# GpSimd's weight work at the head of an attention step, and another order of loads, banks and copies in steps 0 to 3

## The chip, the cores and the metric

The kernel runs on one core of a Trainium2 chip. The time is that of one execution on the device in microseconds (us), as the median of the runs shown. A core has five engines that each work through their own list of instructions in order, and wait for each other by semaphores: TensorE (PE: matrix products, and PEld, which loads their stationary operand), VectorE (DVE), ScalarE (ACT), GpSimd (POOL) and SyncE (SP, which here only issues DMAs). PE writes to PSUM, of which this kernel uses eight banks; DVE and ACT read it out.

## The reference

Causal attention for 4 batches of 12 heads, 448 tokens, head size 64, and behind it a layer with a cosine:

```
scores = q @ k.T / sqrt(64), masked above the diagonal      # per head
attn   = softmax(scores);  x = attn @ v                     # x: (1792, 768)
h   = x @ w_in                                              # (768, 2048)
out = (h * cos(h)) @ w_out                                  # (2048, 768)
```

q, k and v are float32. The weights come as 64-bit floats, two 32-bit words each, and are turned into pairs of float32 parts ("hi" and "lo") on the chip.

## The kernel before, in words

The 48 heads are handled as 24 **pairs** of heads. The function `attention` is a generator; its loop (L489) makes one **step** per iteration and gives control back (`yield`) at the end of each. In step i three pairs are in work, so that no engine waits for one pair's whole chain:

- PE: the scores of pair i (`scores`, L359), the products with v of pair i-2 (`av`, L409), the transposes of q and k of pair i+2 (`transpose_in`, L315), the transposes of the probabilities of pair i-1 (`tp`, L392), the transposes of the output of pair i-2 (`turn_out`, L447). That is its order within a step.
- DVE: masking with the row minimum for pair i (`masked`, seven custom instructions, L368), the division for pair i-2 (`divide`, L436 to L438), and one or two copies of `tp`'s result out of PSUM (`evac_tp`, L319).
- ACT: two copies of the transposed q and k of pair i+1 (`evac_in`, L321), seven exponentials (`exps`, L375), two or three copies of `evac_tp` (L321), two copies for the output of pair i-2 (`finish`, L463 and L464).
- POOL: splits that output into hi and lo (`finish_hi`, L469 and L470).
- SP: four loads of q and k for pair i+3 (`load_qk`, L257) and two of v for pair i-1 (`load_v`, L266), every second step two more of v (L273).

Beside this, between steps (L1342 to L1375), the first weights are prepared in 12 **pieces**, each over two steps. In the first half of a piece DVE makes `ct` from the high words (L139, L142), and POOL squares the high words in place (`hif`, L145). In the second half DVE adds the low words (L148) and multiplies by the test of the squared words against a bound (L152): so **L152 reads what POOL's L145 wrote**. Then POOL makes hi and lo of the result (L156, L157). DVE's part stands in the program at the `yield`, hence ahead of the next step's `masked`. POOL's part is kept in the list `postponed` and issued at the end of the next step, behind that step's `finish_hi` (L557):

```
# in convert_weight, half 0:
    return lambda: nc.gpsimd.tensor_tensor(hif, hif, hif, op=ALU.mult), None
# at the end of a step:
    finish_hi(i - 2, xf)
    while postponed:
        postponed.pop(0)()
    yield i
```

SP also loads the pieces (L117, L122), writes finished weights back to DRAM (`first_halves`, L204 and L206: they wait for POOL's L156 and L157) and raw ones (L1344, behind L152). The pieces start in step 2 and end in step 26. Nothing reorders any of this: the program is recorded under a manual schedule, so each engine's order is that of the Python code.

Ahead of step 0, q and k of pair 0 are transposed with products on zeros (`keep_warm`, L286) before, between and behind. From step 23 on, products of the second part (L567 to L569) fill PE; then the function `moe` runs (from L635), in which PE works almost without a break.

Of the kernel before, what the change touches and what calls it, by code (L numbers as in the profile page):

```python
# [21 lines left out]
def kernel(  # L22
# [15 lines left out]
    nc = tc.nc  # L38
# [189 lines left out]
    def attention(filler_of, postponed):  # L228
        with (
# [6 lines left out]
            NM = S // R  # L236
# [4 lines left out]
            N = len(pairs)  # L241
# [4 lines left out]
            def heads(j):  # L246
                return slice(j * D, (j + 1) * D)

            def half(h):
                return slice(h * R, (h + 1) * R)  # L250

            def load_qk(i, *engs):
                b, hp = pairs[i]
                nat[i] = nat_t[:, i % 3]
                for h, src in ((1, k), (0, q)):
                    for j, eng in enumerate(engs or (nc.sync, nc.sync)):
                        eng.dma_start(  # L257
                            out=nat[i][half(h), :, heads(j)],
                            in_=src[b, 2 * hp + j].rearrange("(p c) d -> p c d", c=NM),
                        )  # L260

            def load_v(i):
                b, hp = pairs[i]
                vn, vo = vals[i] = vn_t[i % 3], vo_t[i // 2 % 2]
                for j in range(2):
                    nc.sync.dma_start(  # L266
                        out=vn[:, :, j, 0:D],
                        in_=v[b, 2 * hp + j, 0:W, :].rearrange("(c p) d -> p c d", p=P),
                    )
                if i % 2 == 0:  # L270
                    for a in range(2):
                        t0 = (LAST[a][1] - 1) * R
                        nc.sync.dma_start(  # L273
                            out=vo[R:P, a].rearrange("p g h e -> p (g h) e")[:, :, 0:D],
                            in_=v[b, 2 * hp : 2 * hp + 4, t0 : t0 + R, :].rearrange("h p d -> p h d"),
                        )
# [3 lines left out]
            load_qk(0, nc.sync, nc.scalar)  # L280
            nc.scalar.copy(cst.tile([P, 32], BF16, name="tab")[:, 0:1], warm[:, 0:1])
            load_qk(1, nc.sync, nc.scalar)

            def keep_warm(n):
                for _ in range(n):
                    nc.tensor.matmul(  # L286
                        banks8[:, 0, 0:P], lhsT=warm, rhs=warm, start=True, stop=True
                    )

            keep_warm(30)  # L290
            ident = cst.tile([P, P], F32, name="ident")
            make_identity(nc, ident)

# [16 lines left out]
            def transpose_in(i, bs, order=None):  # L310
                for h in range(2):
                    qkt[i, h] = flat[:, 2 * h + i % 2, 0:S], banks8[:, bs[h], 0:S]
                for c, h in order or [(c, h) for c in range(NM) for h in range(2)]:
                    o = qkt[i, h][1].rearrange("p (r c) -> p c r", c=NM)
                    nc.tensor.transpose(o[:, c], nat[i][half(h), c], ident[half(h), half(h)])  # L315

            def evac(dst, src, dve=False):
                if dve:
                    nc.vector.tensor_copy(dst, src)  # L319
                else:  # L320
                    nc.scalar.copy(dst, src)  # L321

            def evac_in(i, h, dve=False):
                evac(*qkt[i, h], dve)
# [11 lines left out]
            def col(m):  # L336
                return slice(COL[m], COL[m] + 1)

            def open_step(i):
                prob[i] = prob_t[i % 3]  # L340
                stats[i] = at.tile([P, 8], F32, tag="stat", bufs=3, name="stat")

            def place(m):
                b, o = BANK[m]
                return banks8[:, b, o * R : (o + m) * R]

            def probs(i, m):
                return prob[i][:, AT[m] * R : (AT[m] + m) * R]
# [16 lines left out]
            def masked(i, *ms):  # L365
                for m in ms:
                    z = W if m == TURNED else S - m * R
                    nc.vector.tensor_tensor_reduce(  # L368
                        out=probs(i, m), in0=place(m), in1=mask[:, z : z + m * R], scale=-scale,
                        scalar=3.0e38, op0=ALU.add, op1=ALU.min, accum_out=stats[i][:, col(m)],  # L370
                    )

            def exps(i, *ms):
                for m in ms:
                    nc.scalar.activation(  # L375
                        probs(i, m), probs(i, m), AF.Exp, scale=-1.0, bias=stats[i][:, col(m)]
                    )
# [7 lines left out]
            def open_ptr(i):  # L385
                ptr[i] = at.tile([P, 2, 2, NM, R], F32, tag="pm", bufs=2, name="pm")
# [87 lines left out]
            def fill(n):  # L474
                if not extra:
                    spare = itertools.cycle((7, 6))
                    extra.append(filler_of(lambda: banks8[:, next(spare)]))
                for _ in zip(range(n), extra[0]):
                    pass

            TB_, G1, G2 = (2, 3), (7, 4), (5, 6)
            transpose_in(0, TB_, [(c, 1) for c in range(NM)])
            evac_in(0, 1)
            keep_warm(8)
            transpose_in(0, TB_, [(c, 0) for c in range(NM)])
            evac_in(0, 0, True)
            keep_warm(8)
            load_qk(2)
            for i in range(N + 4):  # L489
                cur, prev, old = i < N, 0 < i <= N, 0 <= i - 2 < N  # L490
                if i >= N - 1:
                    G1, G2 = (2, 3), (4, 5)
                if i + 3 < N:
                    load_qk(i + 3)
                if prev:
                    load_v(i - 1)
                if cur:
                    open_step(i)
                    scores(i)
                if i == 0:  # L500
                    masked(i, 4, 3)
                    exps(i, 4, 3)
                    masked(i, 7, 6)
                    exps(i, 7)
                    transpose_in(1, TB_)
                    evac_in(1, 0, True)
                    evac_in(1, 1)
                    keep_warm(8)
                    exps(i, 6)
                    masked(i, 5, 1, 2)  # L510
                    exps(i, 5, 1, 2)
                    yield i
                    continue
                if i == 1:
                    transpose_in(2, TB_)
                    keep_warm(8)
                    masked(i, 4, 3, 7, 6)
                    evac_in(2, 0, True)
                    masked(i, 5)
                    evac_in(2, 1, True)  # L520
                    masked(i, 1, 2)
                    exps(i, 4, 3)
                elif cur:
                    if i + 1 < N:
                        evac_in(i + 1, 0, i == 2)
                        evac_in(i + 1, 1, i == 2)
                    masked(i, 4, 3, 7, 6, 5, 1, 2)
                    exps(i, 4, 3, 7, 6, 5, 1, 2)
                if i == N + 2:
                    run(extra[0])  # L530
                if old:
                    av(i - 2)
                    divide(i - 2)
                if 1 < i < N - 2:
                    transpose_in(i + 2, TB_)
                if i == N:
                    fill(8)
                if prev:
                    open_ptr(i - 1)
                    tp(i - 1, 0, G1)  # L540
                    evac_tp(i - 1, 0, G1, 0, True)
                    evac_tp(i - 1, 0, G1, 1)
                    if i == 1:
                        exps(i, 7, 6)
                    tp(i - 1, 1, G2)
                    evac_tp(i - 1, 1, G2, 1)
                    evac_tp(i - 1, 1, G2, 0, i % 2 == 0 or i < 4)
                if i == 1:
                    exps(i, 5, 1, 2)
                    transpose_in(3, TB_)  # L550
                if N - 2 < i < N + 2:
                    fill((4, 4, 6)[i + 1 - N])
                if old:
                    turn_out(i - 2)
                    xf = finish(i - 2)
                    finish_hi(i - 2, xf)
                while postponed:  # L557
                    postponed.pop(0)()
                yield i

    def m1_sum(ring, g, fi, t0, n, hv):
# [64 lines left out]
    def run(*gens):  # L626
        for x in gens:
            for _ in x:
                pass
# [699 lines left out]
    with tc.manual_schedule():  # L1329
# [11 lines left out]
        postponed = []  # L1341
# [65 lines left out]
```

## Time and profile before

| what | value |
|---|---|
| time, median of 3 runs | 630.5 us (625.94, 630.5, 631.62) |
| profiled execution: its time / its span | 629.74 us / 627.8 us |
| granted TensorE clock, mean | 0.997 |
| PE busy | 595.1 us (95%) |
| DVE busy | 454.3 us (72%) |
| ACT busy | 402.9 us (64%) |
| POOL busy | 399.0 us (64%) |
| attention steps 0 to 23 begin | 8.17 to 161.83 us |

The span runs from the first to the last instruction; the run's own time is 1.9 us longer. Busy shares are means over very different stages. The part that the change touches is the first 200 us, in which steps follow each other every 5.4 to 8.5 us; a step is cut here at the first instruction of its scores. "Busy" for PE counts a product from its start to a modelled end, so a burst of products that stops and starts again shows more busy time than the same burst in one go.

### The profile page before, as it was taken

What the parts mean: (1) busy time and instruction counts of PE and PEld (TensorE: products, weight loads), DVE (VectorE), ACT (ScalarE), POOL (GpSimd) and SP (SyncE); (2) the same over time, 40 slices, a digit from 0 to 9 for tenths busy, and PEclk for the clock granted to TensorE, in tenths of its full rate; (3) what the DMA queues carried; (4) which work ended last, traced back from release to release, by engine and by line L of the source; (5) the groups of instructions that cost most, each with busy time, mean ns of one, the idle gap of its engine ahead of it and who ended that gap; (6) DMA issues with size and microseconds to landing.
All of it is one profiled execution on the core that took longest, in us unless ns stands there. A gap on an engine that the chain in (4) does not pass through costs nothing.

```text
span 627.8 us, 15322 instructions
## 1 busy us (share of the span) xinstructions
PE 595.1 (95%) x5912; PEld 547.1 (87%) x5912; DVE 454.3 (72%) x957; ACT 402.9 (64%) x783; POOL 399.0 (64%) x426
## 2 busy tenths in 40 slices
PE   8898888886998999999999999999999999999996
PEld 7777777775877998889999999999999999999996
DVE  4877777667638678688777777764358877887886
ACT  3878888867657679687777777743436545644640
POOL 0233343443344978787777777772578788889895
PEclk9999999999999999999999999999999999999999
DMA  8666655754604786978796969669998567548204
GB/s 147 163 141 165 152 139 149 165 129 116 162 3 143 251 307 190 361 238 324 224 329 222 337 199 354 228 231 375 392 363 296 163 241 271 178 160 304 95 1 151
DMA packets 127096, 134.30 MB, mean 214 GB/s; under 512 B 75152, under 2 KB 111360, under 8 KB 127024
## 3 DMA queue, kind: packets, MB, share of 16 engines
q1 hardware_dynamic: 119328, 106.92, 55.2%
q0 software_dynamic: 4928, 24.78, 10.8%
q10 hardware_dynamic: 2768, 1.64, 1.0%
q8 instruction: 46, 0.75, 0.5%
q14 instruction: 26, 0.21, 0.1%
HBM read 83.36 MB, written 49.94 MB: 212 GB/s over the span
## 4 chain that ended last, share of the span: by engine, by line
PE 64%; DVE 20%; ACT 6%; POOL 4%; DMA 3%; issue 3%; SPq 0%; ACTq 0%; DVEq 0%; POOLq 0%
PE banks L663 16%; PE banks L1112 12%; PE banks L1092 11%; DVE pb L368 7%; PE banks L568 5%; PE banks L569 5%; PE banks L567 5%; DVE pm L319 2%; PE banks L409 2%; PE banks L1129 2%; PE banks L1016 2%; DVE on L438 2%; DMA land<-in_moe_w_in_dram 2%; PE banks L359 1%; POOL xa L470 1%
## 5 line engine op out<-in xcount | busy, mean ns | idle before, releaser
L651 DVE TENSOR_TENSOR acc<-acc,banks 128x768 f32<-128x768 f32 (+1 forms) x122 | 112.6, 932 | 43.0 <-PE banks L663 32.9
L663 PE MATMUL banks<-w,gh 128*128 128x384 f32 x512 | 110.3, 336 | 2.5 <-DVE acc L649 1.6
L663 PEld LDWEIGHTS banks<-w,gh 128*128 128x128 f32 x512 | 90.7, 188 | 5.0 <-DVE acc L649 2.0
L375 ACT ACTIVATE pb<-pb,stat 128x256 f32<-128x256 f32 (+6 forms) x168 | 71.8, 498 | 32.5 <-DVE stat L368 32.1
L568 PE MATMUL banks<-xa,w 128*128 128x512 f32 x192 | 75.3, 392 | 0.0
L569 PE MATMUL banks<-xa,w 128*128 128x512 f32 x192 | 75.0, 391 | 0.0
L567 PE MATMUL banks<-xa,w 128*128 128x512 f32 x192 | 74.9, 390 | 0.0
L469 POOL CAST xa<-xf 128x448 fp32r<-128x448 f32 (+1 forms) x18 | 9.7, 539 | 89.0 <-ACT xf L464 89.0
L663 PE MATMUL banks<-w,gl 128*128 128x384 f32 x256 | 65.2, 335 | 0.0
L368 DVE CUSTOM_DVE_ANT_0 pb<-banks,mask 128x256 f32<-128x256 f32 (+6 forms) x168 | 59.8, 418 | 2.6 <-PE banks L359 2.6
L687 POOL TENSOR_TENSOR w<-ct,w 128x768 fp32r<-128x768 f32 x28 | 51.8, 1850 | 15.3 <-ACT w L686 10.0
L575 ACT ACTIVATE ni<-banks 128x512 int32<-128x512 f32 (+1 forms) x64 | 34.5, 538 | 32.6 <-PE banks L569 19.6
L594 POOL TENSOR_TENSOR gl<-r,gh 128x512 fp32r<-128x512 f32 x32 | 41.5, 1298 | 19.0 <-ACT gh L593 18.8
L409 PE MATMUL banks<-vn,pm 128*64 128x65 f32 (+1 forms) x1344 | 49.5, 226 | 1.7 <-ACT xf L464 1.5
L577 DVE SCALAR_TENSOR_TENSOR r<-ni,banks 128x512 f32<-128x512 int32 (+1 forms) x56 | 35.0, 626 | 21.1 <-ACT ni L575 20.3
L409 PEld LDWEIGHTS banks<-vn,pm 128*64 128x64 f32 (+1 forms) x1344 | 45.6, 140 | 3.8 <-ACT xf L464 1.8
L579 ACT ACTIVATE r<-r 128x512 f32<-128x512 f32 (+1 forms) x56 | 32.8, 586 | 25.0 <-DVE r L577 24.4
L663 PEld LDWEIGHTS banks<-w,gl 128*128 128x128 f32 x256 | 46.4, 188 | 0.0
L582 DVE SCALAR_TENSOR_TENSOR r<-r,banks 128x512 f32<-128x512 f32 (+1 forms) x56 | 35.1, 626 | 13.6 <-ACT r L580 13.6
L359 PE MATMUL banks<-flat 64*64 64x64 f32 (+5 forms) x768 | 42.8, 361 | 2.1 <-ACT flat L321 0.6
L1092 PE MATMUL banks<-xb,bb 128*128 128x384 f32 x234 | 44.8, 334 | 0.0
L392 PE MATMUL banks<-ident,pb 64*128 64x64 f32 x672 | 31.9, 228 | 12.2 <-DVE stat L368 12.1
(142 smaller groups left out, 1454.5 us busy)
## 6 DMA issues: line engine op xcount, KB each, us to landing
bb<-w_in_d SPq DMA_DIRECT2D x48, 384.0 KB, 5.0
land<-in_moe_w_in_dram SPq DMA_DIRECT2D x14, 768.0 KB, 6.3
land<-in_moe_w_out_dram SPq DMA_DIRECT2D x14, 768.0 KB, 5.7
w_out_d<-w POOLq DMA_DIRECT2D x14, 768.0 KB, 5.7
big<-w_out_d SPq DMA_DIRECT2D x25, 384.0 KB, 5.0
w_in_d<-w POOLq DMA_DIRECT2D x7, 768.0 KB, 4.1
raw_d<-ct POOLq DMA_DIRECT2D x14, 384.0 KB, 8.0
land<-in_k_dram SPq DMA_DIRECT2D x46, 112.0 KB, 3.4
```

The lines of the kernel that those rows point to most:

```text
L359: nc.tensor.matmul(place(m)[heads(j ^ SWAP[m]), c : c + z - a], lhsT=qt[heads(j), (m - 1) * R : m * R], rhs=kt[heads(j), a:z], start=banks ...
L368: nc.vector.tensor_tensor_reduce(out=probs(i, m), in0=place(m), in1=mask[:, z : z + m * R], scale=-scale, scalar=3.0e38, op0=ALU.add, op1= ...
L375: nc.scalar.activation(probs(i, m), probs(i, m), AF.Exp, scale=-1.0, bias=stats[i][:, col(m)])
L409: nc.tensor.matmul(banks8[half(h), b, c : c + E1], lhsT=lhsT, rhs=rhs, start=start, stop=stop)
L567: yield nc.tensor.matmul(hv, lhsT=wh[:, f], rhs=x[:, 0, cc, t], start=(cc == 0), stop=False)
L568: yield nc.tensor.matmul(hv, lhsT=wh[:, f], rhs=x[:, 1, cc, t], start=False, stop=False)
L569: yield nc.tensor.matmul(hv, lhsT=wl[:, f], rhs=x[:, 0, cc, t], start=False, stop=(cc == NCC - 1))
L651: nc.vector.tensor_tensor(d, d, o, op=ALU.subtract)
L663: nc.tensor.matmul(o[:, e, 0:EH], lhsT=a[:, cs], rhs=w[:, e * EH : (e + 1) * EH], start=(x == 0), stop=(x == 5),)
L687: nc.gpsimd.tensor_tensor(w[:, 1], tf, f32(w[:, 0]), op=ALU.subtract)
L1092: nc.tensor.matmul(o, lhsT=w[:, u, k * P : (k + 1) * P], rhs=x[k][:, v], start=k + m == 0, stop=k == K - 1 and m == 2,)
L1112: nc.tensor.matmul(o[:, b % 2, 0:EH], lhsT=g_ops[i][u][:, c * P : (c + 1) * P], rhs=wouts[g, i][:, v], start=(x == 0), stop=(x == 2),)
```

## The change

1. `postponed` is worked off at the head of the next step instead of at its end. On POOL a piece's instructions now stand ahead of the step's `finish_hi`, not behind it.
2. Ahead of step 0: 44 products on zeros instead of 30, q and k of pair 0 transposed in one alternating series of 14 instead of two series of 7 with 8 products on zeros between them, then 10 products instead of 8.
3. Loads: q, k of pair 2 are issued at the start from SP and ACT; v of pair 0 ahead of step 0 and no v in step 1.
4. Step 1: `tp` of pair 0 goes to banks 0, 1 and 2, 3 (before: 7, 4 and 5, 6). The 8 products on zeros in step 1 are gone. The copies of pair 2's q and k move from DVE to ACT.
5. Pair 3's q and k are transposed in step 2 behind its scores (before: at the end of step 1), and copied by DVE in step 2 behind `masked` (before: ahead of it).

```diff
             load_qk(1, nc.sync, nc.scalar)
+            load_qk(2, nc.sync, nc.scalar)
...
-            keep_warm(30)
+            keep_warm(44)
...
-            TB_, G1, G2 = (2, 3), (7, 4), (5, 6)
-            transpose_in(0, TB_, [(c, 1) for c in range(NM)])
+            TB_ = (2, 3)
+            transpose_in(0, TB_)
             evac_in(0, 1)
-            keep_warm(8)
-            transpose_in(0, TB_, [(c, 0) for c in range(NM)])
             evac_in(0, 0, True)
-            keep_warm(8)
-            load_qk(2)
+            keep_warm(10)
+            load_v(0)
             for i in range(N + 4):
                 cur, prev, old = i < N, 0 < i <= N, 0 <= i - 2 < N
-                if i >= N - 1:
-                    G1, G2 = (2, 3), (4, 5)
+                G1, G2 = (7, 4), (5, 6)
+                if i == 1:
+                    G1, G2 = (0, 1), TB_
+                elif i >= N - 1:
+                    G1, G2 = TB_, (4, 5)
+                while postponed:
+                    postponed.pop(0)()
                 if i + 3 < N:
                     load_qk(i + 3)
-                if prev:
+                if 1 < i <= N:
                     load_v(i - 1)
...
                 if i == 1:
                     transpose_in(2, TB_)
-                    keep_warm(8)
-                    masked(i, 4, 3, 7, 6)
-                    evac_in(2, 0, True)
-                    masked(i, 5)
-                    evac_in(2, 1, True)
-                    masked(i, 1, 2)
+                    masked(i, 4, 3, 7, 6, 5, 1, 2)
                     exps(i, 4, 3)
+                    evac_in(2, 0)
+                    evac_in(2, 1)
+                    exps(i, 7)
                 elif cur:
-                    if i + 1 < N:
-                        evac_in(i + 1, 0, i == 2)
-                        evac_in(i + 1, 1, i == 2)
+                    if 2 < i < N - 1:
+                        evac_in(i + 1, 0)
+                        evac_in(i + 1, 1)
                     masked(i, 4, 3, 7, 6, 5, 1, 2)
                     exps(i, 4, 3, 7, 6, 5, 1, 2)
+                    if i == 2:
+                        transpose_in(3, TB_)
+                        evac_in(3, 0, True)
+                        evac_in(3, 1, True)
...
                     if i == 1:
-                        exps(i, 7, 6)
+                        exps(i, 6, 5)
...
                 if i == 1:
-                    exps(i, 5, 1, 2)
-                    transpose_in(3, TB_)
+                    exps(i, 1, 2)
...
                     finish_hi(i - 2, xf)
-                while postponed:
-                    postponed.pop(0)()
                 yield i
```

How this moves instructions on POOL, from its first output split (step 2) to step 6. The tile `xf` is the output of a pair, `st` a piece's words, `ct` and `w` its results. Before:

```order
L469 CAST xa<-xf 128x448
L470 TENSOR_TENSOR xa<-xf,xa 128x448
L469 CAST xa<-xf 128x448
L470 TENSOR_TENSOR xa<-xf,xa 128x448
L145 TENSOR_TENSOR st<-st 128x256
L469 CAST xa<-xf 128x448
L470 TENSOR_TENSOR xa<-xf,xa 128x448
L156 CAST w_500<-ct 128x256
L157 TENSOR_TENSOR w_500<-ct,w_500 128x256
```

With the change (L470 and L471 are the former L469 and L470):

```order
L470 CAST xa<-xf 128x448
L471 TENSOR_TENSOR xa<-xf,xa 128x448
L145 TENSOR_TENSOR st<-st 128x256
L470 CAST xa<-xf 128x448
L471 TENSOR_TENSOR xa<-xf,xa 128x448
L156 CAST w_500<-ct 128x256
L157 TENSOR_TENSOR w_500<-ct,w_500 128x256
L470 CAST xa<-xf 128x448
L471 TENSOR_TENSOR xa<-xf,xa 128x448
```

Each squaring (L145) and each pair L156, L157 has moved one output split ahead, and so on through all 12 pieces.

PE from the end of step 1's scores to the scores of step 2 and behind them (`land` holds loaded q and k, `pb` probabilities, `vn` v). Before:

```order
L359 MATMUL banks<-flat 64x64 x2
L315 MATMUL banks<-ident,land 128x64 x14
L286 MATMUL banks<-warm 128x128
L392 MATMUL banks<-ident,pb_140 128x64 x28
L315 MATMUL banks<-ident,land 128x64 x14
L359 MATMUL banks<-flat 64x256 x2
```

With the change:

```order
L360 MATMUL banks<-flat 64x64 x2
L316 MATMUL banks<-ident,land 128x64 x14
L393 MATMUL banks<-ident,pb_158 128x64 x28
L360 MATMUL banks<-flat 64x256 x2
```

The product on zeros (eight of them in the program, each with its weight load) and the second series of 14 transposes are gone from between the two scores; the series of 14 stands behind step 2's scores, ahead of the products with v of pair 0.

## Rows read from the trace of the kernel before

**Rows 1.** Waits of DVE, whole span: total us, times, longest

```profile
DVE ct L152 <- POOL st L145: 40.9, 12, 4.1
```

**Rows 2.** Stretches: us, each engine's busy us (x instructions), PEclk, DMA share, GB/s

```profile
63.73:69.10 5.37, 5.30 (x145) 4.76 (x146) 5.18 (x22) 5.20 (x14) 3.07 (x4) 1.00 0.50 119
69.10:77.22 8.12, 6.36 (x146) 5.19 (x146) 4.67 (x21) 5.74 (x15) 2.27 (x3) 1.00 0.68 168
28.86:151.23 122.37, 105.41 (x2610) 89.76 (x2611) 90.04 (x371) 97.81 (x243) 48.94 (x75) 1.00 0.58 140
151.23:161.83 10.60, 7.37 (x132) 6.24 (x132) 4.85 (x21) 6.09 (x16) 2.26 (x3) 0.84 0.86 254
161.83:198.04 36.21, 32.89 (x397) 27.09 (x398) 19.76 (x48) 22.98 (x43) 15.12 (x19) 1.00 0.21 49
4.00:10.00 6.00, 6.00 (x55) 4.79 (x56) 0.62 (x1) 0.53 (x1) 0.00 (x0) 1.00 1.32 190
```

**Rows 3.** Chain of waits in step 10: start us, us, what

```profile
70.37 0.56 POOL xa L469
...
71.01 1.14 POOL xa L470
72.15 0.58 POOL st L145
...
72.75 0.05 DVE ct L152
```

**Rows 4.** Timeline of DVE, steps 9 to 10: start us, us, instruction [idle before <-releaser]

```profile
68.96 0.42 DVE L148 SCALAR_TENSOR_TENSOR ct<-st,ct 128x256 uint32<-128x256 uint32 x1
72.75 0.42 DVE L152 SCALAR_TENSOR_TENSOR ct<-st,ct 128x256 f32<-128x256 f32 x1 [3.38 <-POOL st L145]
```

**Rows 5.** Timeline, DVE's L142 beside POOL's split, in steps 7 and 9

```profile
50.85 0.56 POOL L469 CAST xa<-xf 128x448 fp32r<-128x448 f32 x1 [5.22 <-ACT xf L464]
50.87 0.82 DVE L142 SCALAR_TENSOR_TENSOR ct<-st,ct 128x256 uint32<-128x256 uint32 x1
...
64.44 0.42 DVE L142 SCALAR_TENSOR_TENSOR ct<-st,ct 128x256 uint32<-128x256 uint32 x1
```

**Rows 6.** Timeline of POOL and SP, steps 21 and 22

```profile
148.60 0.39 POOL L156 CAST w<-ct 128x256 fp32r<-128x256 f32 x1
...
149.01 0.34 SPq L204 DMA_DIRECT2D w_out_d<-w  x1
...
151.06 1.28 SPq L273 DMA_DIRECT2D vo<-in_v_dram  x2
```

**Rows 7.** Chain of waits, step 22

```profile
151.72 4.75 DMA vo<-in_v_dram
```

**Rows 8.** Timeline of SP over two steps, first and last of nine rows

```profile
86.70 0.34 SPq L122 DMA_DIRECT2D st<-in_moe_w_out_dram  x1
...
97.50 0.44 SPq L206 DMA_DIRECT2D w_in_d<-w  x1
```

**Rows 9.** Timeline of PE (PEld: weight loads), steps 0 to 3

```profile
1.05 3.38 PE L286 MATMUL banks<-warm 128*128 128x128 bf16 x30 [1.05 <-DVE warm L279]
...
4.36 1.01 PE L315 MATMUL banks<-ident,land 64*128 64x64 f32 x7
...
6.26 0.82 PEld L315 LDWEIGHTS banks<-ident,land 64*128 64x128 f32 x7 [0.20 <-DMA land<-in_q_dram]
...
8.17 2.57 PE L359 MATMUL banks<-flat 64*64 64x256 f32 x32
...
10.68 0.65 PE L315 MATMUL banks<-ident,land 64*128 64x64 f32 x14
...
11.26 0.62 PE L286 MATMUL banks<-warm 128*128 128x128 bf16 x8
...
18.16 1.75 PE L359 MATMUL banks<-flat 64*64 64x256 f32 x32
...
23.50 1.75 PE L359 MATMUL banks<-flat 64*64 64x256 f32 x32
```

## Prediction

> **What bounds the kernel now.** I read the waits of each engine first, then cut the attention into its steps, then followed the chain of waits through one step, because the page's 95% for PE is a mean over a dense second part and a first part that is not dense.
>
> The waits show one line that towers over DVE's others: L152 waits for POOL's L145, 40.9 us in 12 waits, one for each piece of weights [rows 1]. The cut into steps shows what this does. From the start of step 4 to that of step 22 there are 18 steps, nine without such a wait and nine with one, in turn. Step 9 is one without: 5.37 us, and PE is busy for 5.30 of them, so PE fills it. Step 10 is one with: 8.12 us for the same number of PE instructions, and DVE and PE both have room [rows 2]. The chain through step 10 says why: POOL first splits the output of the step before (L469, L470), only then squares (L145), and DVE's L152 starts as L145 ends [rows 3]. DVE has done L148 at 68.96 and stands idle for 3.38 us [rows 4]. Behind L152 in DVE's order are the masks of that step; behind these ACT's exponentials and PE's transposes of probabilities. So the wait is on the path here, and what L152 needs is a squaring that could have run a whole step earlier: its input is ready once L142 is done, and POOL is busy for 3.07 of 5.37 us in step 9 [rows 2].
>
> A second, single loss is step 22: 10.60 us, with the granted clock at 0.84 [rows 2]. There the chain runs through a transfer of v, 4.75 us [rows 7]. It was issued late, at 151.06, because SP had stood at L204, which stores finished weights and starts only as POOL's L156 runs, at 148.60, again behind the split [rows 6].
>
> **The sum, part by part.** It is made against the profiled execution, 629.7 us (its span is 627.8), which is 0.8 us under the median of the runs shown, 630.5.
>
> *POOL's weight work at the head of the step, steps 4 to 21.* No instruction is added; L145, L156 and L157 only change places with L469 and L470. L145 now runs right behind L142, one step ahead of its reader; the squaring takes 0.58 us [rows 3] and the reader comes some 5 us later, so the wait goes whole. Behind POOL's new wait for DVE at a step's head stands only that step's split, whose input comes at the step's end. What is late next is PE. Below 5.37 us a step can't go, since PE's work fills that [rows 2]. The other end: if only PE's idle time came back and its stop-and-go bursts stayed as long as they are, the 18 steps would take PE's busy time, 105.4 us, or 5.86 us a step [rows 2]. I take 5.5, nearer to the short end, because nine steps of the old kernel run at the short pace with all of their DVE and ACT work in them; it is not the very end, because ACT needs 5.20 and 5.74 us in steps 9 and 10 [rows 2], so 5.47 on average, as much as PE, and two engines at their limit that hand banks to each other don't fit without gaps. Sum: 122.4 now [rows 2], 18 x 5.5 = 99.0 then: **23.4 us saved** (17.0 to 25.7).
>
> Do the loads keep up? 140 GB/s over 122.4 us [rows 2] become 140 x 122.4 / 99.0 = 173 GB/s. At the start, where everything waits for q and k, 190 GB/s were moved, and step 10 had 168 without a wait for a transfer [rows 2]. SP needs from 86.70 to 97.94, 11.2 us, for two steps' issues including its waits [rows 8], as against 11.0 us for two new steps. Both are close, and I count nothing for them, because q and k are issued three steps ahead; if 168 were the most, the 18 steps would take 140 x 122.4 / 168 = 102 us, 3 us more than in my sum.
>
> *Step 22.* L156 stands ahead of the split now and can run as soon as L152 is done, one step earlier, so SP comes to L204 and to the v behind it about a step earlier. More than the 4.75 us of the transfer is gained, and the wait goes. The step falls from 10.60 to 5.5, less half a microsecond for the large weight loads that share the queue: **4.6 us** (2 to 5.1).
>
> *Steps 23 to 27.* 36.2 us, of which PE is busy for 32.9 [rows 2], with the filling products of the second part. DVE's two waits there are covered by these; they are worth **0.3 us** (0 to 2).
>
> *Steps 0 to 3.* The 44 products take 44 x 3.38/30 = 5.0 us from 1.05 and end at 6.0, and q lands at 6.26, so they cost nothing [rows 9]. The 14 transposes behind them: at the pace of the old series of 7, 2.0 us; at that of the alternating series of 14 later, 0.65 [rows 9]. The later products on zeros take half as long as the first ones (8 in 0.62 us, as against 30 in 3.38), so I double the 0.65 to 1.3. That ends at 7.6, ten products on zeros end at 8.7, and scores of pair 0 start then instead of at 8.17: 0.5 us lost (0 lost, if the copies end first, to 1.1). Step 1 loses the eight products and the series between the scores, and DVE loses two copies there: some 0.8 us earlier for step 2's scores, which before stood at 18.16. But in step 2 DVE's two copies of pair 3 now stand behind the masks, and a series of 14 ahead of av has to wait until ACT has emptied banks 2 and 3: about what step 1 gave, and step 3's scores come at about 24.0 instead of 23.50 [rows 9]. The early loads of pair 2 and v queue behind those of pairs 0 and 1 on SP and ACT, hence cost nothing. Together **0.5 us lost** (1.5 lost to 1 gained).
>
> Sum: 23.4 + 4.6 + 0.3 - 0.5 = 27.8 us; 629.7 - 27.8 = 601.9, so **602 us**. The ends of the terms together: 629.7 - 33.8 = 596 and 629.7 - 17.5 = 612. All behind the attention only shifts.
>
> **Rivals.**
>
> *GpSimd's work and DVE's get into each other's way.* Step 7's L142 took 0.82 us, the one of step 9 took 0.42; the first started 0.02 us behind POOL's L469 [rows 5]. With the wait gone, L148 and L152 also come to stand beside L469 and L470. Were one of these instructions held for all of L470 (1.14 us [rows 3]) in each step, a step took 5.37 + 1.14 = 6.5 us; the 18 would take 117 and save 5 us, and the sum would be 629.7 - 5 - 4.6 = 620. For it: that row. Against: the split starts when ACT has finished the output, about when DVE begins the head of the next step, and only L142 was ever seen longer; the short steps at 5.37 contain a split and L142 as well. Chance 0.12.
>
> The Trainium skill has this as a rule ("SBUF — State Buffer", section "Who interferes with whom"): a DVE instruction with two inputs in SBUF and a GpSimd instruction that reads SBUF exclude each other for the whole instruction, and the one issued first wins. The trace agrees as far as it goes (0.82 beside a split, 0.42 ahead of one). By the rule the masks, with one input in PSUM, are not touched; the change would lose up to 1.14 us a step, which is the 620 above.
>
> *The wait was not the bound.* If DVE only waits elsewhere, for PE or ACT, steps stay at 6.8 on average, and only step 22 gains: 629.7 - 4.6 = 625. For it: the mean share of PE is 95%. Against: step 9. Chance 0.07.
>
> *Slower: v comes late in every second step.* Steps are shorter, SP issues in order, and ahead of v it has the weight pieces, which wait for DVE, and the stores, which wait for POOL. From the point where SP comes to v less than 4.75 us before PE needs it, step 22 repeats: 9 x (10.6 + 5.4) = 144 us instead of 122.4, which makes 651. For it: SP's 11.2 us for two steps is more than 11.0. Against: those 11.2 contain waits for DVE and PE, which go, and v is issued a step ahead. Chance 0.03.
>
> **How the numbers follow.** My forecast has 0.78, with its own range of 596 to 612. The range that should hold the time 8 times in 10 is 594 to 615: the forecast's ends, a little beyond on either side for the spread of the runs before (0.9% from lowest to highest). A difference under 1%, that is from 624.2 to 636.8 us beside 630.5, I take for none. Faster: the forecast, the first rival, a part of the second: 0.91. Within 1%: most of the second: 0.06. Slower: 0.03.
>
> **What would show it.** In the new profile: no wait of L152 for L145 in steps 4 to 26 (if some stays, POOL is late for another reason); steps of 5.4 to 5.9 us from 4 on, without the alternation; PE's waits for the masks' results in the transposes gone; step 22 like the others, no clock below 1.0 there, and the store at L204 no longer behind the split; scores of step 3 between 22.5 and 25. Wrong would be: L142, L148 or L152 at 0.8 us and more in most steps (first rival), steps still at 8 with another name in front of the wait (second), or PE waiting for v (third).

## The result and the profile after

The changed kernel takes **607.8 us** (median of 4 runs, 604.91 to 608.23), the kernel before 629.9 beside it; the ratio is 0.965, with a 95% interval of 0.959 to 0.970. Forecast was 602 us, with a range of 594 to 615. The gain is real and its size is four fifths of what was forecast: 22 us in place of 28.

The profiled execution took 608.2 us, its span is 606.1, against 627.8 before. The first view is the cut into stretches (us, busy us of PE, PEld, DVE, ACT and POOL with their instructions, PEclk, DMA share, GB/s): all steps 4 to 21, step 13, step 11, step 22, and steps 23 to 27, as in [rows 2].

```profile
27.34:134.87 107.53, 99.59 (x2611) 88.29 (x2611) 91.08 (x371) 96.14 (x243) 48.59 (x75) 1.00 0.71 169
81.73:87.10 5.37, 5.30 (x146) 4.76 (x146) 5.18 (x22) 5.21 (x14) 2.38 (x3) 1.00 0.65 145
69.36:76.35 6.99, 5.77 (x145) 4.98 (x146) 5.19 (x22) 5.22 (x14) 2.42 (x3) 1.00 0.69 161
134.87:140.33 5.46, 5.02 (x132) 4.37 (x132) 4.94 (x21) 5.46 (x15) 2.78 (x4) 1.00 0.59 154
...
140.33:176.50 36.17, 34.00 (x395) 28.58 (x396) 19.24 (x47) 22.71 (x43) 13.57 (x17) 0.95 0.27 71
```

Steps 4 to 21 fell from 122.37 to 107.53 us, 14.8 less; step 22 from 10.60 to 5.46, 5.1 less; the start of step 4 moved from 28.86 to 27.34, 1.5 less; steps 23 to 27 stayed. These make 21.5 of the 21.7 us by which the span fell. The strict alternation of 5.4 and 8.1 us is gone, but it did not turn into 5.4 throughout: ten of the 18 steps take 5.37 to 5.5 us, and the other eight take 5.97 to 7.45.

The wait that was to go has gone. In steps 9 and 10, POOL's squaring now stands well ahead of DVE's L152, which runs behind L148 without a pause, in 0.42 us (timelines of POOL and of DVE; POOL's split is L470 and L471 now):

```profile
57.83 1.15 POOL L471 TENSOR_TENSOR xa<-xf,xa 128x448 fp32r<-128x448 f32 x1
58.93 0.62 POOL L145 TENSOR_TENSOR st<-st 128x256 f32<-128x256 f32 x1
...
61.44 0.41 DVE L148 SCALAR_TENSOR_TENSOR ct<-st,ct 128x256 uint32<-128x256 uint32 x1
61.95 0.42 DVE L152 SCALAR_TENSOR_TENSOR ct<-st,ct 128x256 f32<-128x256 f32 x1
```

What took its place shows in PE's waits from 27 to 135 us (engine, line, whom it waited for: total us, times, longest), and in the chain of waits through steps 10 and 11 (start us, us, what):

```profile
PE banks L410 <- DMA vo<-in_v_dram: 3.7, 5, 1.5
PE banks L410 <- DMA vn<-in_v_dram: 2.4, 4, 0.9
...
62.24 1.72 PE banks L360 x21
...
64.05 0.68 SPq L257
...
64.78 0.62 SPq L257
...
66.11 0.62 SPq L257
...
66.78 0.61 SPq L266
...
67.44 5.13 DMA vn<-in_v_dram
...
72.62 1.92 PE banks L410 x56
```

PE's products of probabilities and v (L410) in step 11 wait for v, v was issued at 66.78 and 67.44, and ahead of it SP had issued four loads of q and k, one behind the other. The first of these took 1.70 us (from 63.03), the other three 0.62 us each. The chain counts only the end of the first, because it takes a signal of PE at 64.05 for the end of a wait; that is hardly one, since the buffer of this load had been free from PE's transposes of step 8 on. Seven of the eight long steps hold such a wait (the eighth, step 9, has 0.6 us for which the trace names nobody). PE's waits of L410 sum to 6.1 us; PE's busy time is 4.0 us longer besides (99.59 us, as against 95.61 where these waits are gone, in experiment 3). Together that is nearly all of the 10.5 us by which these stages exceed 97.0.

SP's own timeline shows that it has no pause left: from 27 to 124 us only two gaps between its issues are longer than 0.2 us (0.44 and 0.25), where the kernel before had nine, of up to 2.7. These are the issues from step 10's first load to step 12's, to be held against [rows 8]:

```profile
63.03 2.37 SPq L257 DMA_DIRECT2D land<-in_k_dram  x2
65.45 1.28 SPq L257 DMA_DIRECT2D land<-in_q_dram  x2
66.78 1.15 SPq L266 DMA_DIRECT2D vn<-in_v_dram  x2
68.02 0.43 SPq L117 DMA_DIRECT2D st<-in_moe_w_in_dram  x1
68.55 1.89 SPq L257 DMA_DIRECT2D land<-in_k_dram  x2
70.49 1.29 SPq L257 DMA_DIRECT2D land<-in_q_dram  x2
71.82 1.40 SPq L266 DMA_DIRECT2D vn<-in_v_dram  x2
73.27 1.27 SPq L273 DMA_DIRECT2D vo<-in_v_dram  x2
74.64 2.19 SPq L257 DMA_DIRECT2D land<-in_k_dram  x2
```

Two steps of issues take 11.6 us here, where two steps of PE could take 2 x 5.37 = 10.7. From the k loads of step 8 (50.60) to those of step 20 (122.46) it is 71.86 us for twelve steps, 12.0 for two: what the steps of PE take, 12.4.

### The profile page after: what moved, and what is told of

Same layout as the page of the kernel before. It is cut to its first block, busy times and chain, and to the rows that moved or that the text cites. A ratio compares the mean times of both kernels' runs of the same rounds, so it can differ in the third digit from the quotient of the medians.

```text
span 606.1 us, 15320 instructions
## 1 busy us (share of the span) xinstructions
PE 587.0 (97%) x5912; PEld 544.5 (90%) x5912; DVE 454.7 (75%) x955; ACT 401.3 (66%) x785; POOL 398.3 (66%) x426
## 4 chain that ended last, share of the span: by engine, by line
PE 73%; DVE 11%; DMA 8%; ACT 3%; SPq 3%; issue 2%; POOL 1%; DVEq 0%; ACTq 0%
PE banks L666 18%; PE banks L1115 12%; PE banks L1095 12%; PE banks L571 6%; PE banks L572 6%; PE banks L570 6%; PE banks L410 4%; PE banks L360 3%; DMA vo<-in_v_dram 2%; DVE pb L369 2%; PE banks L1132 2%; PE banks L1019 2%; DMA vn<-in_v_dram 2%; SPq L257 2%; DVE pm L320 2%
## 5 line engine op out<-in xcount | busy, mean ns | idle before, releaser
L690 POOL TENSOR_TENSOR w<-ct,w 128x768 fp32r<-128x768 f32 x28 | 51.9, 1853 | 16.0 <-ACT w L689 15.9
L470 POOL CAST xa<-xf 128x448 fp32r<-128x448 f32 (+1 forms) x18 | 9.6, 532 | 75.6 <-ACT xf L465 75.6
L410 PE MATMUL banks<-vn,pm 128*64 128x65 f32 (+1 forms) x1344 | 51.3, 227 | 3.9 <-DMA vn<-in_v_dram 2.4
L410 PEld LDWEIGHTS banks<-vn,pm 128*64 128x64 f32 (+1 forms) x1344 | 46.2, 140 | 6.4 <-ACT pb L376 1.9
L360 PEld LDWEIGHTS banks<-flat 64*64 64x64 f32 x768 | 32.7, 133 | 11.4 <-DVE pm L320 3.7
```

The source lines that it names most:

```text
L360: nc.tensor.matmul(place(m)[heads(j ^ SWAP[m]), c : c + z - a], lhsT=qt[heads(j), (m - 1) * R : m * R], rhs=kt[heads(j), a:z], start=banks ...
L410: nc.tensor.matmul(banks8[half(h), b, c : c + E1], lhsT=lhsT, rhs=rhs, start=start, stop=stop)
L690: nc.gpsimd.tensor_tensor(w[:, 1], tf, f32(w[:, 0]), op=ALU.subtract)
```

## The experiments

Each time is a median, and each ratio is to runs of the kernel before that were taken beside it. Three theories were set against each other. **A**: the time that SP needs to issue the loads in order paces the steps, so the number of issues on SP counts. **B**: the transfers pace them, so bytes count, or the landing of the DMA on whose completion an issue waits. **C**: v only has too little lead.

**1. The postponed work alone.** The kernel before, with one edit:

```diff
+                while postponed:
+                    postponed.pop(0)()
                 if i + 3 < N:
                     load_qk(i + 3)
...
-                while postponed:
-                    postponed.pop(0)()
                 yield i
```

> The kernel before with one edit: GpSimd's postponed weight work is issued at the head of a step in place of its end; the head and steps 0 to 3 stay as before. My theory: this edit alone carries the stages 4 to 21 (122.4 us before, 107.5 us after the whole change) and step 22 (10.6 to 5.5 us); steps 0 to 3 stay at 28.9 us, 1.5 us more than with the whole change. So about 609.5 us (607 to 612), VectorE's waits for st gone. Rival: the steps gain only together with the loads and banks moved at the head, since the loads of v stand nearer to their use; then stages 4 to 21 stay over 112 us and the run is at 614 us or more.

Measured: 609.1 us, ratio 0.962 (0.955 to 0.968), the same as of the whole change. Steps 4 to 21 take 107.68 us, step 22 5.46. Its step 10 alone took 9.64 us, at a lower clock (last section). The whole measurable gain is this edit's. Its start of step 4 (27.43) does not stay at 28.9, as I had expected; of that below.

**2. The new head alone.** The changed kernel, with these two lines back at the end of the step (the edit above, in reverse).

> The changed kernel with one edit: GpSimd's postponed weight work is issued at the end of a step again, as before; the new head (44 products, pair 0's q and k transposed together, loads, banks and copies of steps 0 to 3 moved) stays. My theory: the start of step 4 stays at 27.3 us (28.9 before), the stages 4 to 21 go back to 122.4 us and step 22 to some 10.6 us with VectorE waiting for st as before: 628.4 us, 1.5 under the kernel before. Rival: the head's moves carry part of the stages' gain; then stages 4 to 21 are under 119 us and the run is under 625 us.

Measured: 631.9 us, ratio 1.001 (0.996 to 1.006): no difference. DVE's wait is back as in [rows 1], and so are the steps: stretches 4 to 21 and 22, and DVE's waits over the span.

```profile
27.08:151.86 124.78, 107.98 (x2611) 91.75 (x2611) 89.81 (x371) 98.29 (x243) 49.23 (x75) 0.97 0.57 139
151.86:160.25 8.39, 6.87 (x131) 5.89 (x131) 4.97 (x21) 5.77 (x15) 2.26 (x3) 0.82 0.81 227
...
DVE ct L152 <- POOL st L145: 41.6, 12, 4.0
```

The two together settle the attribution: what the head was given carries none of the stages' gain.

**3. Fewer issues, same bytes.** The changed kernel, with one DMA for q (and one for k) of both heads:

```diff
-                    for j, eng in enumerate(engs or (nc.sync, nc.sync)):
+                    if not engs:
+                        nc.sync.dma_start(
+                            out=nat[i][half(h)].rearrange("p c (j d) -> p c j d", j=2),
+                            in_=src[b, 2 * hp : 2 * hp + 2].rearrange("j (p c) d -> p c j d", c=NM),
+                        )
+                        continue
+                    for j, eng in enumerate(engs):
```

> The changed kernel with one edit: from pair 3 on, q and k of a pair are loaded with one DMA each for both heads in place of two, so a step has two DMA issues fewer on SyncE at the same bytes and the same 256-byte rows. Theory A, SyncE's issuing in order is the next bound (11.6 to 11.9 us of issues for two steps, back to back from 9 to 128 us): with 4 issues fewer in two steps, some 2.4 us, SyncE gets ahead, v comes in time, the stages 4 to 21 go from 107.5 to 97 to 100 us and the run to 599 to 601 us. Theory B, the transfers themselves are the bound (169 GB/s in these stages): nothing changes but where SyncE waits; the stages stay at 106 to 109 us and the run at 607 to 609 us.

Measured: **596.2 us**, ratio 0.942 (0.936 to 0.948), under both kernels; the interval lies wholly below that of the changed kernel. Theory A's number came, theory B's did not. The stretch of steps 4 to 21, steps 10 and 11, and SP's issues in step 11 (L272 and L279 are the loads of vn and vo here):

```profile
26.74:123.76 97.02, 95.61 (x2610) 85.71 (x2610) 90.97 (x371) 95.20 (x243) 48.58 (x75) 1.00 0.98 186
59.31:64.68 5.37, 5.30 (x146) 4.76 (x146) 4.85 (x21) 5.37 (x15) 2.78 (x4) 1.00 1.07 210
64.68:70.05 5.37, 5.30 (x145) 4.76 (x145) 5.18 (x22) 5.21 (x14) 2.37 (x3) 1.00 1.06 180
...
66.29 0.60 SPq L257 DMA_DIRECT2D land<-in_k_dram  x1
66.93 0.69 SPq L257 DMA_DIRECT2D land<-in_q_dram  x1
67.67 1.48 SPq L272 DMA_DIRECT2D vn<-in_v_dram  x2
70.89 0.34 SPq L122 DMA_DIRECT2D st<-in_moe_w_out_dram  x1
```

From step 5 on every step takes 5.37 us and PE fills it. An issue of twice the bytes takes about as long as a single one, and SP now has pauses (69.15 to 70.89).

**4. Earlier v.** The changed kernel:

```diff
-                if 1 < i <= N:
-                    load_v(i - 1)
+                if 0 < i < N:
+                    load_v(i)
```

> The changed kernel with one edit: v of a pair is loaded one step earlier (three buffers of vn and two of vo allow it), the number of issues and the bytes unchanged. Theory C, v has only too little lead: its waits vanish, the stages 4 to 21 go from 107.5 to 97 to 101 us, 598 to 602 us. Theory A or B, SyncE's issues or the transfers are too slow as a rate: the wait moves from v to q and k (TensorE's transposes), since the issues of two steps still take 11.6 us and more, where two steps of TensorE take 10.8; the stages stay above 104 us, the run at 604.5 us or more.

Measured: 608.8 us, ratio 0.961 (0.954 to 0.967), no different from the changed kernel; the stages take 111.5 us in the trace, one step of 9.44 us at a lower clock among them. Theory C falls: PE's wait moved from v to q, as a queue that is too slow on the whole would have it (PE's waits, 27 to 138 us):

```profile
PE banks L316 <- DMA land<-in_q_dram: 11.7, 9, 3.3
```

**5. Fewer bytes, same issues.** The changed kernel:

```diff
-                            out=nat[i][half(h), :, heads(j)],
+                            out=nat[i][half(h), 0 : 3 if i > 3 else NM, heads(j)],
...
-                        out=vn[:, :, j, 0:D],
+                        out=vn[:, 0 : 1 if i > 3 else NB, j, 0:D],
```

> The changed kernel with as many DMA issues as before, each smaller: from pair 4 on, q and k are loaded for 3 of 7 row groups and v for 1 of 3 chunks, and the rest of the buffers keeps an earlier pair's values (so the output is not the reference's); two steps then move 640 KB of q, k and v in place of 1408 KB. Theory A, the time of SyncE's issues bounds the stages (a merged issue of 224 KB took 0.60 to 0.69 us, one of 112 KB 0.62, so that time does not hang on the size): the stages 4 to 21 stay at 104 to 108 us, the run at 604 to 608 us. Theory B, transfers or their landing (each issue waits for the DMA eight issues before, and those land after 3.4 to 5.5 us) hold SyncE up: the stages fall to 97 to 99 us, the run to 597 to 600 us. Between them, at 99 to 104 us, both have a share: the issues at 0.62 us each alone would leave some 11.2 us for two steps.

Measured: 604.5 us, ratio 0.961 (0.957 to 0.964). With the DMA share at 0.43 in place of 0.71 the stages still take 105.79 us:

```profile
26.84:132.63 105.79, 100.11 (x2611) 89.07 (x2611) 91.32 (x371) 96.17 (x243) 48.54 (x75) 0.98 0.43 108
```

Q and k landed after 2.4 to 2.5 us there (median; 3.4 to 3.5 in the changed kernel). SP's pace stayed, too: from the k loads of step 8 to those of step 20 it is 11.9 us for two steps, as against 12.0. Fewer than half the bytes, landing a microsecond sooner, are worth 1.7 us of the 10.5 that fewer issues are worth in these stages, and 3.4 of 11.6 in the run. Theory B is out as the main cause in both its forms; a small share of the bytes isn't excluded.

**6. One issue more, same bytes.** The changed kernel:

```diff
-                for j in range(2):
+                for j, c0, c1 in ((0, 0, NB), (1, 0, 2), (1, 2, NB)):
                     nc.sync.dma_start(
-                        out=vn[:, :, j, 0:D],
+                        out=vn[:, c0:c1, j, 0:D],
```

> The changed kernel with one DMA issue more in each step at the same bytes: the second head's v is loaded in two pieces (two chunks and one). Theory A: each issue more costs SyncE some 0.6 us in each of 18 steps, and every step is paced by SyncE: the stages 4 to 21 go from 107.5 to 116 to 119 us, the run to 616 to 620 us. Theory B, the bytes bound: the stages stay at 106 to 110 us, the run at 606 to 611 us.

Measured: 619.2 us, ratio 0.983 (0.978 to 0.988). The stages took 119.45 us and the waits for vo grew from 5 to 14:

```profile
28.43:147.88 119.45, 105.98 (x2611) 93.31 (x2611) 91.36 (x371) 96.43 (x243) 48.43 (x75) 0.96 0.63 151
...
PE banks L410 <- DMA vo<-in_v_dram: 10.9, 14, 1.9
```

119.45 - 107.53 = 11.9 us over 18 steps is 0.66 us for an issue more, nearly the 0.62 us that it takes on SP. In this trace three of these steps ran in part at a lower clock (last section), so the agreement is not exact; but SP's own pace went from 12.0 to 13.4 us for two steps, 0.70 for an issue more.

**7. The merge without the change.** The kernel before, with the edit of experiment 3.

> The kernel before with the merged loads of q and k alone (one DMA for both heads), GpSimd's work still at the end of the step. My theory: the wait for GpSimd's st comes first there and hides the loads, so that the merge changes nothing: stages 4 to 21 at 120 to 125 us, the run at 627 to 632 us. Rival: SyncE held the kernel before up as well; then the stages fall below 117 us and the run below 625 us.

Measured: 630.3 us, ratio 1.001 (0.998 to 1.004). The stages took 128.3 us in the profiled execution, longer than the 120 to 125 I had put down, and the wait for L145 is there (30.3 us from 28 to 152 us). The excess goes with the clock: 0.93 was granted in these stages, and PE was busy for 112.27 us where the kernel before has 105.41. So the merge, worth 11.6 us behind the change, is worth nothing ahead of it: the two limits lay one behind the other, not beside each other.

**8. Another queue.** The changed kernel with vo loaded by GpSimd:

```diff
-                        nc.sync.dma_start(
+                        (nc.gpsimd if i > 3 else nc.sync).dma_start(
                             out=vo[R:P, a]
```

> The changed kernel with the same DMAs at the same bytes, but from pair 4 on the two loads of vo (one step in two) are issued by GpSimd's queue in place of SyncE's. Theory A, it is SyncE's queue that paces the steps, not the number of DMAs: two issues fewer of some 0.63 us leave SyncE some 10.4 us of issues in two steps, under TensorE's 10.75, so the stages 4 to 21 go from 107.5 to 97 to 101 us and the run to 597 to 602 us. Rival: GpSimd's issues of some 0.55 us each stand behind its split and come late, or the number of DMAs counts whoever issues them; then the stages stay at 105 us or more and the run at 605 us or more.

Measured: 608.4 us, ratio 0.961 (0.955 to 0.968), the rival's number. POOL's timeline in step 9, and PE's waits (27 to 136 us), show why:

```profile
58.98 1.15 POOL L471 TENSOR_TENSOR xa<-xf,xa 128x448 fp32r<-128x448 f32 x1
60.09 0.61 POOL L145 TENSOR_TENSOR st<-st 128x256 f32<-128x256 f32 x1
60.65 1.25 POOL L273 DMA_DIRECT2D vo<-in_v_dram  x2
...
PE banks L410 <- DMA vo<-in_v_dram: 4.5, 9, 1.4
```

Step 9 begins at 57.35 there, so vo comes 3.3 us into it, late behind the split. That alone does not tell SP's queue from the number of DMAs, hence the next one.

**9. Another queue, and in time.** As 8, with the loads of vo one step earlier:

```diff
+                if i % 2 == 0 and 3 < i < N:
+                    load_vo(i, nc.gpsimd)
                 if 1 < i <= N:
                     load_v(i - 1)
```

> As the run before with vo on GpSimd's queue, and these loads moved one step earlier (the buffers allow it), so that they no longer come late behind GpSimd's split: there vo was issued 3.3 us into the step, right behind L145, and TensorE waited for it as often as before (4.5 us in 9 waits), while SyncE had time to spare (it waited 9.0 us for VectorE's L152 at L1347). Theory A, it is the place of a load in its queue that paces the steps: the stages 4 to 21 fall from 107.5 to 97 to 101 us, the run to 597 to 602 us, at the same DMAs and bytes. Rival: the number of DMAs in all counts, whoever issues them (each waits for the one eight before): the stages stay at 105 us or more, the run at 605 us or more.

Measured: 598.7 us, ratio 0.950 (0.943 to 0.957). As many DMAs and bytes as in the changed kernel, and the stages take 98.94 us. Neither half of it does that alone: v earlier on SP's queue gave 608.8 us (4), GpSimd's queue without the lead 608.4 (8). Of PE's waits for v none is left:

```profile
28.26:127.20 98.94, 96.96 (x2611) 86.55 (x2611) 90.97 (x371) 95.53 (x243) 59.43 (x93) 1.00 0.88 185
```

So neither the DMAs nor their bytes held the steps up, but the place of each in SP's order. The Trainium skill ("DMA: Bandwidth & Descriptors", section "Rules for kernel authors") says that spreading DMAs over several issuing engines brings no bandwidth and saves only issue time on the sequencer. These runs agree on the issue time: it was what was short, and one issue fewer on SP per step was worth 8.6 us of 107.5. They don't test the bandwidth.

## Why the prediction was right, and where it was off

*The wait goes whole: right.* L152 no longer waits for L145 in any step, and experiments 1 and 2 show that this edit alone makes the measured gain.

*18 x 5.5 = 99.0 us, 23.4 saved: the mechanism was right, the size was not.* It measured 107.5, 14.8 saved, below the low end of that term (17.0). The step of it that failed is "Do the loads keep up?", where I wrote that "both are close, and I count nothing for them". My own row said that SP needs 11.2 us for two steps [rows 8], and I set it against 11.0 for two new ones: a queue that is slower than its consumer paces it, by however little. I discounted it because those 11.2 us held waits that would go and because q and k are issued three steps ahead. The lead can only put such a loss off, since in the new kernel SP no longer gains on PE in long steps. And the pace did not get shorter: it became 11.6 to 12.0 us. With the loads relieved (experiments 3 and 9) the 18 steps take 97.0 and 98.9 us, 5.39 and 5.50 us a step, so the term was right for all else. My reason for 5.5 in place of 5.37 was not: in experiment 3 ACT was as full as I had said (95.20 of 97.02 us), PE too (95.61), and from step 5 on the steps took 5.37 all the same.

The range held in spite of this term, which was 8.6 us too good and came out 2.2 below its own low end. The start of the kernel, 2.0 us better than I had it and for the most part not by the change, and step 22, 0.5 better, made up for some of it; without them the time would have been some 610 us.

I also looked for the limit in the wrong place. I worked out GB/s (173 against 168 and 190) and took transfers for the thing that might not keep up; experiment 3 moved 186 GB/s in these stages, and experiment 5 shows that bytes mattered little at 169. What counted was the time of the issues: 0.60 to 0.69 us for most loads of q and k, whether of 48, 112 or 224 KB, and longer ones among them (below).

*The third rival was this mechanism, priced in the wrong way.* I gave "v comes late in every second step" a chance of 0.03 and 651 us, by repeating step 22 nine times. It came, with the sign that I had named for it (PE waiting for v), in seven of 18 steps, but these were only 0.9 to 2.1 us over 5.37: the wait is as long as SP has fallen behind, not as long as a whole transfer. A rival that is right in kind and far too dear takes weight from a mild form of itself that should have stood in the sum. Worked out mildly, from 11.2 us for two steps, the 18 steps would have been 9 x 11.2 = 101 us.

*Step 22: right.* 5.46 us, 5.1 saved (4.6 forecast), clock at 1.00. SP's L204 still stands ahead of the loads of v, but these come at 130.1 (vo), 4.8 us before step 22 begins.

*GpSimd's and DVE's work in each other's way: it appeared, and cost nothing.* In 11 of the 12 pieces L142 runs beside the split's first instruction (L470). L142 starts 0.12 to 0.29 us ahead, keeps its 0.42 to 0.43 us, and it is L470 that takes up to 0.72 us where a free one takes 0.56:

```profile
56.91 0.42 DVE L142 SCALAR_TENSOR_TENSOR ct<-st,ct 128x256 uint32<-128x256 uint32 x1
57.03 0.71 POOL L470 CAST xa<-xf 128x448 fp32r<-128x448 f32 x1 [2.86 <-ACT xf L465]
...
63.56 0.56 POOL L470 CAST xa<-xf 128x448 fp32r<-128x448 f32 x1 [4.01 <-ACT xf L465]
```

The reverse came once: L152 at 28.26 us started 0.08 us behind L470 and took 0.75. The kernel before has both, too [rows 5]: started 0.01 us ahead, L142 took 0.42 us and the split's first instruction 0.83 (four of five times); started 0.01 to 0.02 behind, L142 took 0.56 to 0.83 (five times). So whichever started first kept its time, as that rival had it. But the rival priced the collision by L470 of the kernel before (1.14 us) in each step, and DVE stood behind a split in one of 36 cases; POOL, busy for 48.59 of 107.53 us, has room for its part.

*Steps 0 to 3: sign wrong, within the range.* 1.5 us earlier in these two profiles, where I had 0.5 lost. Most of that is not the change's: experiment 1 has the old head and starts step 4 at 27.43. Its first scores took 1.75 us, those of the kernel before took 2.57 in that one execution [rows 9]. From the scores of step 1 to those of step 4 the old head takes 16.4 us (16.40 to 16.42 in three profiles), the new one 15.94 in the changed kernel and 15.8 to 15.9 in five of the experiments (16.9 in experiment 9, 17.6 in 6):

```profile
6.38 0.73 PE L316 MATMUL banks<-ident,land 64*128 64x64 f32 x14 [0.59 <-DMA land<-in_q_dram]
7.04 0.73 PE L287 MATMUL banks<-warm 128*128 128x128 bf16 x10
7.89 1.75 PE L360 MATMUL banks<-flat 64*64 64x256 f32 x32
...
11.40 1.75 PE L360 MATMUL banks<-flat 64*64 64x256 f32 x32 [0.62 <-ACT flat L322]
...
15.36 1.75 PE L360 MATMUL banks<-flat 64*64 64x256 f32 x32
...
21.96 1.75 PE L360 MATMUL banks<-flat 64*64 64x256 f32 x32
```

Step 1 got 1.7 us shorter (3.96 for 5.70; I had 0.8), step 2 1.3 longer (6.60 for 5.34; I had about as much as step 1 gave). The 14 transposes together took 0.73 us, not 1.3: the doubling was wrong also by its own rows, since 30 products in 3.38 us and 8 in 0.62 are 0.113 and 0.078 us each, a factor of 1.45. Half a microsecond gained is less than the times can tell from none.

*Steps 23 to 27: 0.0 measured, 0.3 forecast.*

What stays open: 14 loads at 0.62 us, some three weight pieces at 0.4 and 17 gaps of 0.05 between them make 10.7 us for two steps, but SP's pace is 11.6 to 12.0. Some issues take 0.9 to 1.9 us (2.37 and 1.89 for two, above), and they do so at less than half the bytes too (a load of k of 48 KB took 1.95). Without them SP and PE would have been just even: from 27 to 124 us the changed kernel has 18 issues over 0.8 us among its 129, together 13.8 us longer than 0.61 each. The list of DMA packets in the traces holds a lead to their cause. Queue 8, whose packets the profile calls "instruction", moves 46 of 16 KB in the whole run, one for about 257 of PE's 11,824 products and weight loads (one for 255 from 27 to 127 us), so I take it for the queue of PE's code:

```profile
q8 instruction: 46, 0.75, 0.5%
```

Of the 18 long issues 17 overlap such a packet, of the 111 others 14. In experiments 1, 4, 5, 6 and 8 it is all 89 of the long ones, in 3 and 9 it is 40 of 47. That they fall together is shown; why an issue on SP should take longer then, no run here tested.

## What to carry over

When a wait goes, price the next limit by the slowest thing that everything passes in order, queues that only issue DMAs among them: count its issues per step, multiply by the time of one, add what its long issues cost, and compare with the step you hope for; a shortfall of 2% is a pace, not "close". A load's lead hides only a delay that doesn't repeat, so an earlier issue on a full queue moves the wait (v to q), while fewer issues, or another queue that is in time, take it away. And a second limit that is hidden is worth nothing by itself: the merged loads gave 0 us ahead of the change and 11.6 behind it.

## What the hardware showed that I had not expected

The time of an issue on SP does not follow the bytes: loads of q and k took about 0.62 us at 112 KB, 0.60 to 0.69 at 224 KB and 0.60 to 0.61 at 48 KB (medians), while the loads of weight pieces of 256 KB took 0.34 to 0.44 in the kernel before and the changed one.

With the loads merged, the DMA share of the stages was 0.98 (in single steps above 1) and PE still waited for none of them.

A step can lose more than its waits. In experiment 1, PE waited 1.0 and 1.2 us for v in step 10; from 66.79 us on the granted clock was at the lower of its two levels, 1.2 in place of 2.4 GHz, for 3.41 us; the step took 9.64 us, and the same number of PE instructions kept PE busy for 7.48 us where 5.30 is usual at 1.00:

```profile
61.16:70.80 9.64, 7.48 (x146) 6.58 (x146) 4.94 (x21) 5.44 (x15) 2.76 (x4) 0.82 0.81 186
```

Steps 4 to 21 hold one such stretch of 3.41 us also in the profiles of experiments 4 and 5, two in that of 2, three in that of 6 and five in that of 7; they hold none in the kernel before, the changed kernel and experiments 3, 8 and 9. So their times compare the clock, too.
